# Twelve V-cache loads issued from the ACT queue in place of the SP queue, in a decode attention kernel

## The chip, the cores and the metric

The kernel runs on one core of a Trainium2 chip. The metric is the device time of one execution in microseconds (us). "Span" is the profiled execution's own length, some 1.7 us less than its time.

## The reference, cut to what matters

```python
def _A_ref(x, k_cache, v_cache, wq, wo):          # one token, 32 query heads on 4 KV heads
    q = (x @ wq) ...                              # wq 1024 x 4096
    scores = einsum(q, repeat(k_cache, 8)) * 128 ** -0.5    # caches 4 x 65536 x 128, bf16
    o = einsum(softmax(scores), repeat(v_cache, 8))
    return o @ wo
# ... B is an MLP with w1, w2 (1024 x 1024), w3 (1024 x 3584), w4 (3584 x 1024)
return x + _A_ref(xn, ...) + _B_ref(xn, ...)
```

The two caches are 67.1 MB each and every byte is read once. With the weights, 169.87 MB come from HBM for one token.

## The kernel before: the parts that matter

K and V are read in 16 blocks each (K0 to K15, V0 to V15) of 4 MiB, 128 partitions x 32 KiB, into two buffers each (`Kn`, `Vn`). A block serves two of the 32 steps. A third buffer, `W`, takes one weight load at a time. Every load but that of x (2 KB, from ACT) is issued by SP, in program order; each issue waits until the compute has freed the buffer.

```python
def issue_kv(t, b_t, cache, m, ch):
    ...
    s = m % 2
    src = cache[0, h, ...].rearrange("(p c) d -> p (c d)", p=P)
    if m < NPAIR - 1:
        _dma(q_sp, chan(...), lambda e: e.dma_start(out=t[:, s, :], in_=src), writes=b_t[s])
    else: ...                                     # the last block comes in two halves
...
for n in range(NT):                               # 32 steps
    QK(n)                                         # PE
    Ttr(n + 1, [0])                               # DVE transposes a quarter of the next K half block
    stats1(n); ...; EXP(n)                        # DVE, ACT
    Ttr(n + 1, [1]); PTr(n); Ttr(n + 1, [2, 3])
    PV(n)                                         # PE; after an odd n its V buffer is free
    FLASH(n)                                      # ACT copies OT_ps, POOL accumulates
    if n in at_pe:
        at_pe[n]()                                # n = 3, 7, ..: weight matmuls; after 3 and 15 a gelu,
                                                  # which has a tanh on ACT
    if n in at_dma:
        at_dma[n]()                               # n = 0, 4, 8, ..: next weight load
    if n % 2 == 0:
        issue_k(n // 2 + 2)
    else:
        issue_v(n // 2 + 2)
```

DVE works in order, so `Ttr(n + 1, [0])` before `stats1(n)` holds an odd step n until the next K block has landed. And each engine's queue works in order: a load issued from a queue goes out only when everything before it in that queue has been dispatched (seen below: V9 goes out at 239.72 us, together with the tanh before it).

## Time and profile before

| | before |
|---|---|
| time, median | 403.76 us |
| span | 401.9 us |
| bytes | 169.87 MB |
| DVE, PE, ACT busy | 57%, 48%, 12% |
| mean rate over the span | 423 GB/s |

From the profile page of the kernel before, parts 2 and 3. The first two lines cut the span into 40 slices: busy share of the 16 DMA engines in tenths, and GB/s. The last is the queue of the SP ring: packets, MB, share of the 16 engines' span.

```profile
DMA  8999999999999999999999999999999999999994
GB/s 356 427 416 436 444 421 419 450 432 421 444 434 423 432 434 439 416 434 452 423 420 450 426 424 444 432 421 435 430 435 427 445 430 424 424 431 430 436 419 205
...
q1 hardware_dynamic: 6920, 169.87, 98.4%
```

The engines are full from the second slice to the last but one. The table by stretches shows the same for two stretches (columns: stretch, its length, busy time of each engine, granted clock, DMA share, GB/s):

```profile
core 0: us, PE busy (x) PEld busy (x) DVE busy (x) ACT busy (x) POOL busy (x), PEclk, DMA share, GB/s
88.00:100.00 12.00, 4.85 (x39) 1.30 (x35) 8.99 (x17) 1.87 (x5) 1.98 (x2) 1.00 1.00 430
228.00:260.00 32.00, 20.17 (x172) 8.86 (x171) 21.89 (x40) 4.53 (x12) 4.38 (x5) 0.55 1.01 434
```

DVE does wait for K, by the list of waits (engine, line, tile, whom it waited for: us in total, times, longest):

```profile
DVE X L464 <- DMA Kn<-in_A_k_cache_dram: 64.2, 11, 9.9
```

While it waits, the DMA engines are not idle. This is a kernel bound by the bytes, and the compute merely waits its turn.

### The profile page before, as it was taken

What the parts mean: (1) busy time and instruction counts of PE and PEld (TensorE: products, weight loads), DVE (VectorE), ACT (ScalarE), POOL (GpSimd) and SP (SyncE); (2) the same over time, 40 slices, a digit from 0 to 9 for tenths busy, and PEclk for the clock granted to TensorE, in tenths of its full rate; (3) what the DMA queues carried; (4) which work ended last, traced back from release to release, by engine and by line L of the source; (5) the groups of instructions that cost most, each with busy time, mean ns of one, the idle gap of its engine ahead of it and who ended that gap; (6) DMA issues with size and microseconds to landing.
All of it is one profiled execution on the core that took longest, in us unless ns stands there. A gap on an engine that the chain in (4) does not pass through costs nothing.

```text
span 401.9 us, 5169 instructions
## 1 busy us (share of the span) xinstructions
PE 193.7 (48%) x2059; PEld 83.0 (21%) x2059; DVE 227.8 (57%) x400; ACT 48.3 (12%) x127; POOL 61.8 (15%) x90
## 2 busy tenths in 40 slices
PE   0361446064525756286640965454443645445645
PEld 0250111021103511062110731121111311111232
DVE  0217666277816588255753388576836775788410
ACT  0000201012101011011110011111201111111200
POOL 5000013011211011110310102111110112112110
PEclk9999999999955565555565556565565855665686
DMA  8999999999999999999999999999999999999994
GB/s 356 427 416 436 444 421 419 450 432 421 444 434 423 432 434 439 416 434 452 423 420 450 426 424 444 432 421 435 430 435 427 445 430 424 424 431 430 436 419 205
DMA packets 7088, 170.20 MB, mean 423 GB/s; under 512 B 916, under 2 KB 920, under 8 KB 1048
## 3 DMA queue, kind: packets, MB, share of 16 engines
q1 hardware_dynamic: 6920, 169.87, 98.4%
q8 instruction: 16, 0.26, 0.2%
q14 instruction: 8, 0.07, 0.0%
q10 hardware_dynamic: 144, 0.00, 0.0%
HBM read 169.87 MB, written 0.00 MB: 423 GB/s over the span
## 4 chain that ended last, share of the span: by engine, by line
DMA 54%; DVE 22%; PE 17%; ACT 3%; issue 2%; SPq 0%; POOL 0%; ACTq 0%
DMA Kn<-in_A_k_cache_dram 43%; DVE X L464 11%; DMA Kn<-in_B_w_dram 6%; DMA Vn<-in_A_wq_dram 5%; PE H_ps L367 4%; DVE pT_f L517 3%; PE S_ps L476 3%; PE OT_ps L524 3%; DVE mrow L483 3%; ACT p_sb L506 3%; PE M_ps L367 2%; PE PT_ps L515 2%; PE M_ps L552 1%; PE OUT_ps L392 1%; DVE Yall L381 1%
## 5 line engine op out<-in xcount | busy, mean ns | idle before, releaser
L464 DVE STREAM_TRANSPOSE X<-Kn 128x1024 f32<-128x1024 f32 x128 | 151.7, 1215 | 64.2 <-DMA Kn<-in_A_k_cache_dram 64.2
L524 PE MATMUL OT_ps<-Vn,pT_f 128*32 128x512 bf16 x512 | 59.9, 620 | 27.2 <-DVE pT_f L517 27.2
L476 PE MATMUL S_ps<-X,Yall 128*32 128x512 bf16 x512 | 57.5, 593 | 17.0 <-DVE X L464 17.0
L489 PE MATMUL MB_ps<-Rm,Lmat 128*128 128x16 bf16 x32 | 6.1, 192 | 87.3 <-DVE Rm L484 87.3
L538 POOL TENSOR_TENSOR O_acc<-O_acc,tmpO 128x513 f32<-128x513 f32 x28 | 32.9, 1174 | 89.0 <-ACT tmpO L532 89.0
L506 ACT ACTIVATE p_sb<-S_ps,brun 128x512 bf16<-128x512 f32 x32 | 22.0, 687 | 172.3 <-DVE brun L504 153.8
L536 POOL TENSOR_SCALAR O_acc<-O_acc,ff 128x513 f32<-128x513 f32 x28 | 19.5, 698 | 149.8 <-ACT ff L511 149.8
L515 PE MATMUL PT_ps<-p_sb,permR 128*128 128x512 bf16 x32 | 18.2, 568 | 39.7 <-ACT p_sb L506 39.7
L483 DVE TENSOR_REDUCE mrow<-S_ps 128x1 f32<-128x512 f32 x32 | 21.6, 674 | 24.2 <-PE S_ps L476 24.2
L532 ACT ACTIVATE tmpO<-OT_ps 128x512 f32<-128x512 f32 x32 | 19.1, 598 | 107.6 <-PE OT_ps L524 107.6
L476 PEld LDWEIGHTS S_ps<-X,Yall 128*32 128x32 bf16 x512 | 16.5, 125 | 54.8 <-DVE X L464 38.6
L517 DVE STREAM_TRANSPOSE pT_f<-PT_ps 128x512 f32<-128x512 f32 x32 | 22.9, 716 | 7.6 <-PE PT_ps L515 7.6
L524 PEld LDWEIGHTS OT_ps<-Vn,pT_f 128*32 128x32 bf16 x512 | 14.5, 127 | 59.2 <-DVE pT_f L517 42.4
L489 PEld LDWEIGHTS MB_ps<-Rm,Lmat 128*128 128x128 bf16 x32 | 3.3, 102 | 111.2 <-DVE Rm L484 111.2
L367 PEld LDWEIGHTS H_ps<-xn_bf,W 128*128 128x128 bf16 x224 | 14.4, 174 | 1.7 <-issue 1.7
L367 PE MATMUL H_ps<-xn_bf,W 128*128 128x1 bf16 x224 | 14.5, 202 | 0.0
L515 PEld LDWEIGHTS PT_ps<-p_sb,permR 128*128 128x128 bf16 x32 | 3.4, 106 | 42.4 <-ACT p_sb L506 42.4
L493 DVE TENSOR_REDUCE Bst<-MB_ps 128x1 f32<-128x16 f32 x32 | 5.6, 174 | 8.3 <-PE MB_ps L489 8.3
L331 PE MATMUL M_ps<-ln_s,ones_f 128*128 128x1 f32 x6 | 1.8, 363 | 17.5 <-DVE ln_s L330 17.5
L534 POOL COPY O_acc<-tmpO 128x513 f32<-128x513 f32 x4 | 2.4, 612 | 47.6 <-ACT tmpO L532 47.6
L392 PE MATMUL OUT_ps<-Kn,gh_bf 128*1 128x256 bf16 x112 | 6.4, 402 | 5.5 <-DMA Kn<-in_B_w_dram 5.5
L619 DVE CAST orow<-OUT_ps 128x256 bf16<-128x256 f32 x1 | 0.4, 425 | 13.2 <-PE OUT_ps L392 13.2
(101 smaller groups left out, 117.3 us busy)
## 6 DMA issues: line engine op xcount, KB each, us to landing
Kn<-in_A_k_cache_dram SPq DMA_DIRECT2D x15, 4096.0 KB, 27.5
Vn<-in_A_v_cache_dram SPq DMA_DIRECT2D x15, 4096.0 KB, 22.2
W<-in_B_w_dram SPq DMA_DIRECT2D x2, 3584.0 KB, 24.9
W<-in_A_wo_dram SPq DMA_DIRECT2D x3, 2048.0 KB, 24.3
Kn<-in_A_wq_dram SPq DMA_DIRECT2D x1, 4096.0 KB, 12.2
Vn<-in_A_wq_dram SPq DMA_DIRECT2D x1, 4096.0 KB, 21.4
W<-in_B_w_dram SPq DMA_DIRECT2D x2, 2048.0 KB, 32.1
Kn<-in_A_k_cache_dram SPq DMA_DIRECT2D x2, 2048.0 KB, 24.9
```

The costliest lines, as they stand in the source:

```text
L367: fns.append(lambda e, j=j, cx=cx: e.matmul(ps_tile[:, c0 + cx:c0 + cx + 1], lhs_fn(j - j0, cx), rhs_fn(j), start=(j == 0 and cx == 0), st ...
L392: fns.append(lambda e, lhs=lhs, rhs=rhs, jj=jj: e.matmul(OUT_ps[32 * jj:32 * jj + 1, 0:256], lhs, rhs[:, 256 * jj:256 * jj + 256], start=F ...
L464: _op(q_dve, lambda e, ix=ix: e.transpose(out=X32[:, xs, 1024 * ix:1024 * (ix + 1)], in_=Kn32[:, s, 4096 * half + 1024 * ix:4096 * half + ...
L476: fns.append(lambda e, we=we, cm=cm, mv=mv: e.matmul(S_ps[32 * cm:32 * cm + 32, :], Yall[:, h, we, :, :].rearrange("p a g -> p (a g)"), mv ...
L483: _op(q_dve, lambda e: e.reduce_max(mrow[:, m:m + 1], S_ps[:, :], axis=AX.X), reads=[b_S], writes=[b_mrow[m]])
L506: _op(q_act, lambda e: e.activation(p_sb[:, m, :], S_ps[:, :], ACTF.Exp, bias=brun[:, kn:kn + 1], scale=SCALE, accum_out=tmpO[:, m, 512:513]),
L515: _op(q_pe, lambda e: e.matmul(PT_ps[:, :], permR[:, :], p_sb[:, m, :], start=True, stop=True), reads=[b_p[m], b_const], writes=[b_PT])
L517: _op(q_dve, lambda e: e.transpose(out=pT_f[:, :], in_=PT_ps[:, :]), reads=[b_PT], writes=[b_pT])
L524: fns.append(lambda e, q=q, q4=q4: e.matmul(OT_ps[32 * q4:32 * q4 + 32, :], pT_bf[:, q, :, 1], Vn[:, s, 8192 * half + 512 * q:8192 * half ...
L532: _op(q_act, lambda e: e.activation(tmpO[:, m, 0:512], OT_ps[:, :], ACTF.Copy), reads=[b_OT], writes=[b_tmpO[m]], partial=True)
L536: _op(q_pool, lambda e: e.tensor_scalar(out=O_acc[:, :], in0=O_acc[:, :], scalar1=ff[:, m:m + 1], scalar2=0.0, op0=ALU.mult, op1=ALU.add), ...
L538: _op(q_pool, lambda e: e.tensor_tensor(out=O_acc[:, :], in0=O_acc[:, :], in1=tmpO[:, m, :], op=ALU.add), reads=[b_tmpO[m]], writes=[b_Oacc])
```

## The change

The intent was to have two rings of loads feed each DMA engine, in the hope that the engine finds work in one ring while the other is between loads. V2 to V13 go to ACT's queue; the first and last V blocks, all of K and all weights stay on SP.

```diff
-        def issue_kv(t, b_t, cache, m, ch):
+        def issue_kv(t, b_t, cache, m, ch, q=None):
+            q = q or q_sp
...
-                _dma(q_sp, chan("%s%d" % (ch, s)), ...)
+                _dma(q, chan("%s%d" % (ch, s)), ...)
...
-            issue_kv(Vn, b_V, A_v_cache, m, "v")
+            issue_kv(Vn, b_V, A_v_cache, m, "v", q_act if 2 <= m < NPAIR - 2 else q_sp)
```

More of the change, by code (lines that the diff above doesn't have):

```diff
@@ L286, in issue_kv @@
             if m < NPAIR - 1:
-                _dma(q_sp, chan("%s%d" % (ch, s)), lambda e: e.dma_start(out=t[:, s, :], in_=src), writes=b_t[s])
+                _dma(q, chan("%s%d" % (ch, s)), lambda e: e.dma_start(out=t[:, s, :], in_=src), writes=b_t[s])
             else:
```

## The prediction

> **What bounds the kernel now.** The 16 DMA engines. The table of stretches shows a DMA share of 1.00 and 432 GB/s in every stretch from 10 to 300 us; the page shows queue q1 (the SP ring) with 169.87 MB and 98.4% of the engines' span. No compute engine is near that (DVE 57%, PE 48%). In the packet records a 32 KiB packet takes 1213 ns at the median, the 5th and the 95th percentile, a 16 KiB packet 611 ns: 9 ns plus bytes at 27.2 GB/s per engine, 435 GB/s for 16. That is the 435 GB/s that the Trainium skill ("DMA: Bandwidth & Descriptors", Specifications) gives as the fabric ceiling; this trace agrees. The bytes alone need 169.87 MB / 432 GB/s = 393 us of the 402 us span; the rest is about 3 us of start and 4 us after the last loads.
>
> The SP ring is never short of work: by the timeline's issue times and sizes, at each issue 6.9 us (at 241 us) to 32 us of transfer are still queued. DVE's waits for K in the list of waits (64.2 us, 11 times) are full engines, not late issues.
>
> **What the change removes, adds, moves.** 12 loads of 4 MiB, 50.3 MB or 30% of the bytes, move to ACT's ring (q10), with 12 issues of 0.33 us. ACT is busy 12%; an issue stands right after the copy of OT_ps, which already waited for the PV that frees the V buffer, so ACT waits for nothing new, and its idle 3.3 us or more before the next exponential take up the 0.33 us. Nothing is removed from the 393 us.
>
> *Gain possible:* a second ring can hide at most the 9 ns per packet, 0.7% of the shared stretch, under 2 us. The same page ("Issuing engines are not separate DMA queues") says that DMAs of several issuers run on the same 16 engines and interleave, saving only sequencer time. I expect that.
>
> *Loss possible:* K no longer has the engines alone, and V is fetched before it is needed. With equal sharing (my estimate from 432 GB/s, the issue order, 8.1 us per step and the measured weight-matmul extras) K lands some 6 us later relative to the bytes moved, most of all behind a W load; the issues that hang on K come later and the queued reserve shrinks by as much. Its minimum near 241 us, and the end near 370 us, then come close to zero, with perhaps 1 us of idle engines in all. The last flash step ends some 4 us later (381 now); PE has about 5 us of slack before the last W4 load at 399 us, so this stays hidden, just.
>
> **On the critical path:** nearly nothing: the bytes and the rate per engine stay.
>
> **Prediction: 404.0 us, range 401.5 to 408.5.** Faster by over 2%: 0.02; within 2%: 0.92; slower by over 2%: 0.06.
>
> **What the profile would show.** q10 with about 50 MB, q1 about 119.5; 428 to 436 GB/s from 10 to 360 us; 32 KiB packets of two rings that take about twice 1213 ns or alternate at 1213; DVE waits for K still 60 to 75 us, single ones over 10 us after a W load; V landing before it is needed.
>
> **What would make it wrong.** Packets of two rings that together exceed 27.2 GB/s per engine (faster); a switching cost per packet: 50 ns would be 4% of the shared stretch (slower); unfair sharing, K far below half, which empties both rings while compute waits (slower); a compute end more than 5 us later.

## More of the kernel before

Last, the timeline of the kernel before around V9's issue, lines of other work left out (start, length, engine, line, operation, in brackets the idle time before it and its releaser):

```profile
221.67 1.90 PE L524 MATMUL OT_ps<-Vn,pT_f 128*32 128x512 bf16 x16 [0.81 <-DVE pT_f L517]
223.50 7.26 PE L367 MATMUL H_ps<-xn_bf,W 128*128 128x1 bf16 x112
223.62 0.60 ACT L532 ACTIVATE tmpO<-OT_ps 128x512 f32<-128x512 f32 x1 [3.33 <-PE OT_ps L524]
223.68 0.33 SPq L287 DMA_DIRECT2D Vn<-in_A_v_cache_dram  x1
231.68 0.23 ACT L412 ACTIVATE ge_a<-ge_b 128x28 f32<-128x28 f32 x1 [7.46 <-DVE ge_b L411]
```

V9 goes out at 223.68 us, right after the PV of step 15 has freed its buffer. The weight matmul (7.26 us) and the tanh of the gelu come after it.

## The result, and the profile after

The changed kernel takes 413.53 us (median of 5 runs, 411.90 to 414.02), the kernel before 403.76 us (5 runs, 403.68 to 404.60). The ratio is 1.0232, 95% interval 1.0211 to 1.0253: slower. The profiled run has a span of 410.2 us, 8.3 us more than before. It is the fastest of the five (411.90 us); the median run is 1.6 us longer, and no trace of it was kept.

The same lines of the page, after:

```profile
DMA  8999999998999999999999969999999999999994
GB/s 358 409 457 407 447 419 441 430 438 318 435 428 441 416 429 431 447 419 433 432 428 436 419 268 414 455 412 430 434 446 425 414 412 435 409 425 432 449 414 206
...
q1 hardware_dynamic: 5192, 119.54, 68.3%
q10 hardware_dynamic: 1872, 50.33, 28.7%
```

The bytes moved to q10 as intended. Two slices stand out, the tenth (318 GB/s) and the 24th (268 GB/s). The table by stretches:

```profile
88.00:100.00 12.00, 6.53 (x99) 3.01 (x99) 9.05 (x23) 1.90 (x6) 1.79 (x2) 0.50 0.82 325
228.00:260.00 32.00, 22.36 (x223) 12.84 (x224) 21.18 (x39) 4.01 (x12) 4.19 (x5) 0.55 0.88 369
```

The DMA engines, which were never idle before, now run dry: the share falls from 1.00 to 0.82 and from 1.01 to 0.88. Adding up the bytes of the packet records per microsecond against 432 GB/s, what was not moved amounts to 2.6 us at 94 to 98 us, 4.3 us at 235 to 241 us, and 1.3 us in three smaller places (near 190, 329 and 339 us): 8.2 us in all, out of the 8.3 us that the span grew. So in this run that sum is where the time went. The rate of a busy engine did not change: a 32 KiB packet still takes 1213 ns at the median and at the 5th and 95th percentile, on either ring.

Three more views say how the engines came to run dry. First, the chain that ended last, the piece for K2 (start, length), before and then after:

```profile
49.95 27.53 DMA Kn<-in_A_k_cache_dram
```

```profile
49.87 37.02 DMA Kn<-in_A_k_cache_dram
```

K2 is issued at the same time (49.9 us) and lands 9.4 us later. Second, the wait of DVE for K after the change: fewer waits, and the longest doubled.

```profile
DVE X L465 <- DMA Kn<-in_A_k_cache_dram: 72.6, 8, 18.8
```

The longest is the wait for K2, by the timeline:

```profile
86.91 1.25 DVE L465 STREAM_TRANSPOSE X<-Kn 128x1024 f32<-128x1024 f32 x1 [18.81 <-DMA Kn<-in_A_k_cache_dram]
```

Third, the timeline around V9's issue, after, with the same lines left out:

```profile
229.71 1.90 PE L525 MATMUL OT_ps<-Vn,pT_f 128*32 128x512 bf16 x16 [0.81 <-DVE pT_f L518]
231.54 7.26 PE L368 MATMUL H_ps<-xn_bf,W 128*128 128x1 bf16 x112
231.66 0.60 ACT L533 ACTIVATE tmpO<-OT_ps 128x512 f32<-128x512 f32 x1 [3.33 <-PE OT_ps L525]
238.88 0.33 SPq L447 DMA_DIRECT2D W<-in_A_wo_dram  x1
239.72 0.23 ACT L413 ACTIVATE ge_a<-ge_b 128x28 f32<-128x28 f32 x1 [7.45 <-DVE ge_b L412]
239.72 0.33 ACTq L288 DMA_DIRECT2D Vn<-in_A_v_cache_dram  x1
```

The PV that frees V9's buffer ends at 231.6 us, but the issue stands behind the tanh in ACT's program and goes out with it at 239.72 us, 8.1 us late. V3 stands behind the tanh of the first gelu in the same way: ACT's copy is at 93.89 us, the tanh at 96.47, the issue at 96.48. On SP neither had to wait for a tanh. Both late issues fall in the two stretches that run dry. That suggested the first theory below. Alone it turned out not to be enough.

### How the shares of the rings can be read

The packet records tell how many bytes each ring moved. In GB/s, from the changed kernel and from three experiments that are described below:

| kernel | stretch, us | waiting on SP (row) | on ACT (row) | SP ring | ACT ring | SP's share |
|---|---|---|---|---|---|---|
| after | 66 to 70 | W1 (16 KiB) | V2 (32 KiB) | 133.5 | 297 | 0.31 |
| after | 76 to 80 | K2 (32 KiB) | V2 (32 KiB) | 246 | 187 | 0.57 |
| k_halves_first | 74 to 76 | K2 (16 KiB) | V2 (32 KiB) | 139 | 294 | 0.32 |
| halves_first | 76 to 80 | K2 (32 KiB) | V2 (16 KiB) | 300 | 132 | 0.69 |
| quarters_first | 76 to 80 | K2 (32 KiB) | V2 (8 KiB) | 334 | 98 | 0.77 |

The sum stays at 430 to 433 GB/s, but the shares follow the row sizes: 16 against 32 KiB gives about a third, equal rows about a half, 32 against 8 KiB about four fifths. (The 0.57 for equal rows is over a half because V2's last packets start between 75.6 and 79.2 us: on some engines the ACT ring ran empty within the stretch.) The Trainium skill ("DMA: Bandwidth & Descriptors", section "Queues, rings and completion order") says that each engine takes turns between the queue rows it has work for, a whole packet at a time. This trace agrees, with a turn here as large as one row of the load. A ring with smaller rows is therefore served with fewer bytes.

K2's own lateness does not come from these shares. Its 9.4 us are nearly the whole transfer of V2 (4 MiB at 432 GB/s, 9.7 us): V2's last packet ends at 80.5 us, before K2 lands at 86.9, so V2, W1 and K2 had all been moved by then, and at equal shares K2 would have landed no earlier. Halving K's rows moves it as little: in k_halves_first, where K takes half of V's turn, K2 lands at 86.9 us too. Only shares that leave part of V2 unmoved help it, as in quarters_first, where it lands at 81.7 us.

The packet records show one more thing about a ring that was empty. When the other ring still has much queued, the first packet of a new load starts 3.4 to 4.1 us after its issue (V2: issued at 59.96, first packet at 63.44 us; V8: 209.25 and 212.72); when the engines have run dry, it starts after 0.95 to 0.98 us. Why is not shown.

### The profile page after: what moved, and what is told of

Same layout as the page of the kernel before. It is cut to its first block, busy times and chain, and to the rows that moved or that the text cites. A ratio compares the mean times of both kernels' runs of the same rounds, so it can differ in the third digit from the quotient of the medians.

```text
span 410.2 us, 5141 instructions
## 1 busy us (share of the span) xinstructions
PE 185.1 (45%) x2043; PEld 82.8 (20%) x2059; DVE 227.8 (56%) x400; ACT 48.3 (12%) x127; POOL 61.8 (15%) x90
## 4 chain that ended last, share of the span: by engine, by line
DMA 51%; DVE 25%; PE 18%; issue 2%; ACT 2%; another core or an unknown queue 1%; SPq 0%; POOL 0%; ACTq 0%
DMA Kn<-in_A_k_cache_dram 40%; DVE X L465 13%; DMA Kn<-in_B_w_dram 5%; DMA Vn<-in_A_wq_dram 5%; PE S_ps L477 4%; PE H_ps L368 4%; DVE pT_f L518 3%; DVE mrow L484 3%; PE OT_ps L525 3%; PE M_ps L368 2%; ACT p_sb L507 2%; PE PT_ps L516 1%; PE M_ps L553 1%; PE OUT_ps L393 1%; DVE Rm L485 1%
## 5 line engine op out<-in xcount | busy, mean ns | idle before, releaser
L465 DVE STREAM_TRANSPOSE X<-Kn 128x1024 f32<-128x1024 f32 x128 | 151.3, 1214 | 72.6 <-DMA Kn<-in_A_k_cache_dram 72.6
L516 PE MATMUL PT_ps<-p_sb,permR 128*128 128x512 bf16 x16 | 9.1, 566 | 21.2 <-ACT p_sb L507 21.2
L553 PE MATMUL M_ps<-O_acc,cb_W 128*128 128x128 f32 x32 | 6.5, 364 | 2.0 <-DVE cb_W L546 2.0
```

The lines of the kernel that those rows point to most:

```text
L465: _op(q_dve, lambda e, ix=ix: e.transpose(out=X32[:, xs, 1024 * ix:1024 * (ix + 1)], in_=Kn32[:, s, 4096 * half + 1024 * ix:4096 * half + ...
L516: _op(q_pe, lambda e: e.matmul(PT_ps[:, :], permR[:, :], p_sb[:, m, :], start=True, stop=True), reads=[b_p[m], b_const], writes=[b_PT])
L553: fns.append(lambda e, t=t: e.matmul(M0_ps[:, 128:256], cb_W[:, t, :, :].rearrange("p g i -> p (g i)"), O_acc[:, t * P:(t + 1) * P], start ...
```

## The experiments

All against the kernel before, run beside it on the same chip. The diffs shown are against the changed kernel, except that of one_ring_late. "Not moved" is the sum described above, between 40 and 345 us, of the profiled run.

| run | time, median us | ratio to before (95% interval) | span, us | not moved, us |
|---|---|---|---|---|
| before | 403.7 to 403.9 | 1 | 401.9 | 0 |
| after | 413.53 | 1.0232 (1.0211 to 1.0253) | 410.2 | 8.2 |
| v_first | 410.88 | 1.0177 (1.0162 to 1.0192) | 409.2 | 6.7 |
| v9_first | 408.87 | 1.0123 (1.0108 to 1.0138) | 407.1 | 4.5 |
| one_ring_late | 403.98 | 1.0008 (0.9993 to 1.0023) | 402.9 | 0.6 |
| v_halves | 407.33 | 1.0086 (1.0069 to 1.0103) | 405.7 | 3.8 |
| act_only | 403.77 | 0.9996 (0.9980 to 1.0013) | 402.3 | 0 |
| halves_first | 406.10 | 1.0048 (1.0027 to 1.0069) | 404.8 | 1.3 |
| quarters_first | 405.37 | 1.0035 (1.0018 to 1.0052) | 403.6 | 0 |
| k_halves_first | 413.17 | 1.0242 (1.0212 to 1.0272) | 411.6 | 8.6 |
| early_halves | 406.67 | 1.0069 (1.0054 to 1.0084) | 404.5 | 2.2 |
| w_act | 407.15 | 1.0093 (1.0053 to 1.0134) | 405.4 | 2.9 |
| halves_from3 | 404.30 | 1.0014 (0.9997 to 1.0031) | 402.3 | 0 |

One of the four runs of quarters_first was slow (413.39 us, with no lower granted clock than the others; why is not known) and is left out of its ratio. Outputs were correct in all runs.

### First set: late issue or shared engines?

Theory 1: the loss comes from the late issues of V3 and V9 behind the tanh, on a reserve of queued loads that sharing has made thin. Theory 2: the sharing alone is enough. Theory 3: two rings make packets slower.

**v_first**: V is issued before the weight matmuls of its step.

```diff
+            if n % 2 == 1:
+                issue_v(n // 2 + 2)
             if n in at_pe:
                 at_pe[n]()
...
-            else:
-                issue_v(n // 2 + 2)
```

> The changed kernel with each V load issued before the weight matmuls and the gelu of its step instead of after them, so that the loads of V3 and V9 no longer stand behind a tanh in ACT's order (96.48 and 239.72 us in the changed kernel, where the PV that frees the buffer ended at 93.8 and 231.6). Theory 1 (late issue behind the tanh, on a reserve that sharing has thinned): the idle of the DMA engines at 94 to 98 us and 235 to 241 us nearly goes, 404 to 406.5 us, DMA share 0.99 to 1.00 in both stretches. Theory 2 (the sharing of the engines between K and V alone delays K and starves the rings; the tanh is beside the point): unchanged, 411 to 414 us. Theory 3 (two rings make packets slower): unchanged too.

Measured: 410.88 us. It lies between the theories: the lateness is gone (V3 at 93.96, V9 at 235.52 us, the tanhs at 96.54 and 243.58), but only 2.65 of the 9.8 us come back. The two stretches in v_first:

```profile
88.00:100.00 12.00, 6.52 (x99) 3.00 (x99) 9.06 (x23) 1.83 (x6) 1.79 (x2) 0.50 0.97 396
228.00:260.00 32.00, 20.39 (x207) 12.36 (x208) 21.00 (x40) 3.95 (x11) 3.11 (x4) 0.50 0.90 370
```

The first is mended in part (325 to 396 GB/s). In the second one idle place has become two, at 234 to 238 and 251 to 255 us, with 2.2 and 2.6 us not moved. Theory 1 falls as the whole explanation.

**v9_first**: only V9 is issued early (`if n == 15: issue_v(...)` before `at_pe`; the others stay).

> Only V9 is issued before the weight matmul and gelu of step 15; V3 stays behind its tanh. Theory 1: the idle near 238 us (about 4.4 us worth of bytes) goes and the one near 96 us (about 2.6 us) stays: 407.5 to 410 us. Theories 2 and 3: 411 to 414 us.

Measured: 408.87 us, inside theory 1's range, and in the places that it named: the one at 94 to 98 us stayed (2.8 us), the one at 235 to 241 us is gone, and 1.7 us are left from 230 us on. V9 now goes out right after ACT's copy:

```profile
232.61 0.60 ACT L533 ACTIVATE tmpO<-OT_ps 128x512 f32<-128x512 f32 x1 [3.33 <-PE OT_ps L525]
232.62 0.34 ACTq L288 DMA_DIRECT2D Vn<-in_A_v_cache_dram  x1
```

And yet it is faster than v_first, which mends V3 as well. With V3 late the later blocks met each other in a different order: K8 landed at 225.6 us with 11.0 us queued, against 228.5 us and 6.6 us in v_first. How much is lost in one place depends on the phases of K, V and the weights, and does not add up change by change.

**one_ring_late**: the kernel before, with the same lateness put in.

```diff
         def issue_v(m):
+            if m in (3, 9):
+                q_sp.wait(tanh_ev[0])      # the event of the gelu's tanh
```

> The kernel before (all loads on the SP ring) with the same lateness put in: SP waits for the tanh before it issues V3 (2.5 us later) and V9 (8 us later). Theory 1 says both parts are needed: the one ring still held 10.5 us of transfer at V3's issue and 9.6 us at V9's, more than the delays, so the engines stay busy: 403.5 to 405 us, DMA share 1.00 in 90 to 100 and 220 to 250 us. If lateness alone is the cause, whatever the rings: 408 us or more.

Measured: 403.98 us, 0.6 us not moved. On one ring 8 us of lateness costs next to nothing: V9 went out at 231.8 us with 2.0 us of transfer still queued, as the sum said (10.1 us queued when it goes out on time, less 8.1).

**v_halves**: the order of the changed kernel, but each V load on ACT is two loads of 16 KiB rows, so that V's turn is half of K's.

```diff
+            if q is q_act:
+                for hf in range(2):
+                    _dma(q, chan(...), lambda e, hf=hf: e.dma_start(out=t[:, s, 8192 * hf:8192 * hf + 8192],
+                         in_=src[:, 8192 * hf:8192 * hf + 8192]), writes=[b_t[s][hf]])
```

> The changed kernel, order kept (V3 and V9 behind the tanh), but each V load of the ACT ring cut into two loads of 16 KiB rows, so that a turn of the ACT ring is 16 KiB and one of the SP ring 32 KiB for K and 16 KiB for W: K should get about two thirds of the engines while both rings hold work, and W a half in place of a third. Theory 2: most of the loss goes, 404 to 406.5 us. Theory 1: K lands earlier, so the reserve is larger, but V3 and V9 are as late: a part goes, 406 to 410 us. Theory 3: unchanged or slower (about 1 us for 96 more packets per engine at 9 ns).

Measured: 407.33 us: a part goes, though the late issues stay. Tilting the turns alone gives back 6.2 of 9.8 us, more than taking away the lateness does (2.65 us in v_first, 4.7 us in v9_first).

So the four corners are: one ring, 403.7 us; one ring with late issues, 404.0; two rings with timely issues, 410.9; two rings with late issues, 413.5. Lateness costs 0.2 us on one ring and 2.6 us on two. Sharing with timely issues costs 7.1 us. By these corners theory 2 has the larger part. The split is not a firm one, though: v9_first, with V3 still late, is 5.1 us above the kernel before, so mending V9 alone gives back 4.7 of the 9.8 us. What is shown is that lateness costs next to nothing without sharing, and that sharing costs several us without lateness. Theory 3 falls by the packets, which take 1213 ns as before.

### Second set: is it the sharing, and which way?

Theory A: two rings share each engine, K lands later and less is queued when the next issue is due. Theory B: ACT as the issuer costs.

**act_only**: K2 to K13, V2 to V13 and the weight loads between them all go on ACT's ring, in the old order, V issued first in its step.

```diff
-            issue_kv(Kn, b_K, A_k_cache, m, "k")
+            issue_kv(Kn, b_K, A_k_cache, m, "k", q_act if 2 <= m < NPAIR - 2 else q_sp)
...
+                wq[0] = q_act if n >= 4 else q_sp     # queue of the weight loads
                 at_dma[n]()
+                wq[0] = q_sp
```

> K and V blocks 2 to 13 and the weight loads between them all go on the ACT ring, in the order of the kernel before (V issued before the weight matmuls of its step); the rest stays on SP. One ring holds nearly everything again, but it is ACT that issues. Theory A (what costs is that two rings share each engine: K lands with less queued behind it, 6.6 to 14.9 us of transfer against 12 to 22 before, and the next load cannot be issued until 7 us after K lands): back to the time before, 403.5 to 405.5 us. Theory B (the cost lies in ACT as the issuer, its in-order queue or its ring): stays at 409 us or more.

Measured: 403.77 us, ratio 0.9996. ACT issues 30 loads in place of 13, and nothing is lost:

```profile
88.00:100.00 12.00, 7.22 (x80) 2.34 (x77) 9.23 (x18) 1.68 (x5) 1.98 (x2) 0.50 1.01 436
228.00:260.00 32.00, 20.71 (x176) 9.15 (x175) 21.91 (x40) 4.54 (x12) 4.39 (x5) 0.55 1.01 433
```

Theory B falls: issuing from ACT, or using its ring, is not what costs. Having two rings is.

**halves_first**: v_first and V in two loads of 16 KiB rows.

> Both mends at once: V issued first in its step, and each V load of the ACT ring cut into two of 16 KiB rows so that K gets two thirds of the engines while both rings hold work. Theory A: K lands earlier, more stays queued at its landing; better than either alone, 404.5 to 407 us. If the turns of the rings are not what matters: as v_first, 410 to 411.5 us.

Measured: 406.10 us, inside the range, with 1.3 us not moved.

**quarters_first**: the same with four loads of 8 KiB rows.

> The same with V in four loads of 8 KiB rows: K gets about four fifths. Theory A: K about as early as on one ring, at the cost of about 2.5 us for 288 more packets per engine at 9 ns each, part of it off the idle time; V now comes last and PV may wait for it (it did, 21 us in all, in v_halves): 405 to 408.5 us.

Measured: 405.37 us, and nothing is left unmoved; the rest over the kernel before is about the cost of the added packets. By the fit of 9 ns plus bytes at 27.2 GB/s, 288 more packets per engine are 2.6 us (an estimate from the packet durations of the kernel before); the span grew by 1.7.

**k_halves_first**: the opposite tilt. K's loads on SP are cut into two of 16 KiB rows (compute waits for both), V stays whole.

> The opposite tilt, on v_first: each K load of the SP ring cut into two of 16 KiB rows (compute still waits for both), V kept at 32 KiB, so that V gets two thirds. Theory A: K lands later still, less stays queued, more idle engines than v_first: 412 to 419 us. If only the number of rings or the extra packets matter: 410.5 to 412 us.

Measured: 413.17 us, inside theory A's range though near its lower end:

```profile
88.00:100.00 12.00, 6.52 (x99) 3.00 (x99) 9.05 (x23) 1.82 (x6) 1.79 (x2) 1.00 0.99 395
228.00:260.00 32.00, 19.53 (x192) 11.90 (x192) 19.39 (x38) 3.95 (x11) 3.10 (x4) 0.50 0.91 376
```

With V issued in time in all four, the time follows K's turn against V's: 413.2 us at 1:2, 410.9 at 1:1, 406.1 at 2:1, 405.4 at 4:1, and 403.8 on one ring. Cutting loads costs packets in each of the three cut kernels, so it is the tilt that separates them.

### Third set: what is left

**early_halves**: as halves_first, but the first half of a V block is issued a step earlier, as soon as its half of the buffer is free.

> As halves_first (V in two loads of 16 KiB rows on the ACT ring, before the weight matmuls), but the first half of a V block is issued one step earlier, as soon as the PV of its first half frees the buffer. The sharing is that of halves_first; only the reserve grows: half a V block (2 MiB, 4.9 us of transfer) can already be queued when K lands. Theory A (idle engines come from a thin reserve at K's landing): the rest of the idle (1.3 us at 94 to 100 in halves_first) goes, 403.5 to 405 us. If the remaining 2.3 us of halves_first are a cost of two rings or of more packets themselves: stays at 405.5 to 406.5 us.

Measured: 406.67 us, a miss. The idea was to have more queued when K lands. But an early V half is also more V in front of K: K2 landed at 92.0 us in place of 85.9 in halves_first, with 7.9 us queued against 9.1, and 2.2 us were not moved against 1.3. On two rings a load issued earlier takes turns from the one that is waited for.

**w_act**: v_first with the weight loads moved to ACT's ring too.

> v_first (whole V loads of 32 KiB rows on ACT, issued first), with the weight loads moved to the ACT ring as well, so that K is alone on the SP ring and no weight load stands in front of it. Theory A: K no longer waits behind a weight load that gets only a third to a half of the engines, so it lands earlier with more queued: 404.5 to 408 us against 410.9 for v_first. If the equal turns of K and V alone make the loss: 410 to 412 us.

Measured: 407.15 us (one run 409.67), inside theory A's range; so about half of what v_first loses has to do with the weight loads being on K's ring. Moving them also puts them in front of V, and this run cannot tell the two apart. K2 was not helped, though: it landed at 87.0 us all the same, with 8.0 us queued, which is less than K3 alone, so V2 and W1 had both been moved before it; and PE now waited 40.9 us for V, six times.

**halves_from3**: halves_first with V2 back on SP (`3 <= m` in place of `2 <= m`).

> halves_first with V2 back on the SP ring, so that V2 no longer takes two thirds to a half of the engines while W1 and K2 wait on SP. Theory A: K2 lands at about 77.5 us as in the kernel before (not 85.9), 17 us of transfer stay queued at its landing, and the idle of 1.3 us at 94 to 100 us, the only one left in halves_first, goes; what then remains over the kernel before is about 1 us for 88 more packets per engine: 404.3 to 405.5 us. If two rings cost by themselves: 406 us as halves_first.

Measured: 404.30 us, ratio 1.0014 (0.9997 to 1.0031). K2 lands at 77.3 us with 17.8 us queued, and the last idle place is gone. So two rings can be tuned until they cost about nothing. No version of them beat the kernel before, and neither did one ring on ACT.

### The sum that gives the idle time

Why does late K make the engines run dry, when the bytes are the same? Because the next issue hangs on K. After K lands, DVE transposes, and it is 7.0 us until PV has ended and V's next load can be issued (K2 lands at 86.9 us, ACT's copy that follows PV starts at 93.89). With the engines dry, the first packet starts 0.95 to 0.98 us after an issue. So at K's landing some 8 us must be queued (an estimate from these two), or another issue must come meanwhile. The landings come from the semaphore records, "queued" is bytes issued less bytes moved, at 432 GB/s:

| kernel | K lands, us | queued, us | queue ends, us | next issue, us | its first packet, us | not moved, us |
|---|---|---|---|---|---|---|
| before, K2 | 77.5 | 17.6 | 95.1 | V3 at 84.5 | (not idle) | 0 |
| before, K8 | 216.6 | 17.1 | 233.7 | V9 at 223.7 | (not idle) | 0 |
| after, K2 | 86.9 | 8.2 | 95.1 | W2 at 95.71 | 96.66 | 2.6 |
| after, K8 | 224.7 | 11.9 | 236.6 | wo0 at 238.88 | 239.85 | 4.3 |
| v_first, K8 | 228.5 | 6.6 | 235.1 | V9 at 235.52 | 236.50 | 2.2 |

(The engines finish and start about a microsecond apart from each other, so the lost bytes do not equal the gap exactly.) One row does not run dry for want of reserve alone: after, K8 has 11.9 us queued, more than 8. There V9 could have gone out at 231.66 us, with ACT's copy and some 5 us still queued; it is the tanh, 8.1 us later, that let the engines run dry. On one ring K8 had 17.1 us queued, and the same lateness cost 0.6 us (one_ring_late). Before, with everything in one ring in the order of need, K lands with V of the same block and the next K both still to come: 17 us. With two rings, V has been moved while K was on its way, and that much less is left. Put in one number, the least transfer that was queued at any issue between 45 and 350 us: 7.4 us before, none in the changed kernel and in v_first, 2.1 us in halves_first, 6.7 us in halves_from3.

## Why the prediction was wrong, point by point

- **What bounds the kernel, and the rate**: right. The bytes at 432 GB/s bound it, a second ring hid nothing of a packet's 1213 ns, and packets of two rings alternate with the same sum. The prediction drew here on the Trainium skill ("DMA: Bandwidth & Descriptors", section "Issuing engines are not separate DMA queues"); the trace agrees: 430 to 433 GB/s with both rings busy.
- **Direction of the loss**: the mechanism was named. K lands later relative to the bytes, the queued reserve shrinks, worst behind a weight load and near 241 us. K2's single wait went to 18.8 us ("over 10 us after a W load"), and the sum of the waits, 72.6 us, lies in the stated 60 to 75.
- **The step that failed: "with perhaps 1 us of idle engines in all."** It measured 8.2 us. Timely issues on two rings alone (v_first) leave 6.7 us. The prediction counted the reserve at issues on one ring (its least was 6.9 us, 7.4 us by the count used here) and subtracted a delay of K of some 6 us. That delay was mis-sized where it mattered: relative to the bytes moved, K2 landed 9.5 us later, all of V2, while K8 landed 5.2 us later. The reserve that matters is the one at K's landing, against the 7.0 us of compute and 0.96 us of first packet until the next load can start. The stretch at 94 to 98 us, which K2 makes dry, was not seen at all. Sharing was also taken as equal in bytes, whereas a ring with 16 KiB rows got 0.31 of the bytes against 32 KiB rows; for K2 this made no difference, as said above.
- **A second step that failed: "so ACT waits for nothing new."** That holds for ten of the twelve loads. V3 and V9 stand behind the gelu's tanh in ACT's order and went out 2.6 and 8.1 us after PV. Undoing this gives 2.65 us (413.53 to 410.88), and undoing it for V9 alone 4.7 us (v9_first, 408.87). The order of instructions per engine, which was there to be read, shows both.
- **The end**: right that it stays hidden. The changed kernel's span grew by 8.3 us, and 8.2 us of that are unmoved bytes before 345 us.
- **Time**: 404.0 us predicted, range 401.5 to 408.5, measured 413.53. The chance given to "slower by over 2%" was 0.06. One of the listed causes of an error, rings that both run empty while compute waits, is what happened; the share needed for it was not "far below half", as K2 had 0.57 once it stood at the head of its ring.

What stays open: how the losses divide between single places. v9_first beat v_first though it mends less, and no run explains each later place one by one.

## What to carry to other kernels

When the DMA engines are full, as here, a second ring brings no bandwidth (430 to 433 GB/s with both rings busy, 432 with one); it only changes the order in which bytes arrive, from the order of need to taking turns. Keep loads that the compute waits for next ahead of loads that it needs later, and check how much transfer is queued when the awaited load lands against the time until the next issue can follow. If a load must go on a compute engine's queue, look at what stands before it in that engine's program, and remember that a load with smaller rows got the smaller share here (0.31 for 16 KiB beside 32 KiB).

## What the Trainium skill lacked or had wrong

- "DMA: Bandwidth & Descriptors", rules for kernel authors: it says that spreading loads over several issuers does not help. It does not say that it can cost: 403.76 to 413.53 us with the same bytes, of which 5.1 to 7.1 us remain when V9 or all V loads are issued in time (v9_first, v_first).
- The same page, "Queues, rings and completion order": turns go by packet, but nothing is said of shares. Here they followed the row size of the load: 0.31 for 16 KiB against 32 KiB rows, about a half (0.57) for equal ones, 0.77 for 32 against 8 KiB.
- The same page, Specifications: first-byte latency of about 0.6 us for loads issued from SP or ACT; the row does not say from when it counts. With idle engines the first packet's record starts 0.95 to 0.98 us after the start of the issuing instruction, and 0.63 to 0.65 us after its end (it takes 0.33 us), so the figure agrees if counted from the end. Behind a busy other ring the first packet comes 3.4 to 4.1 us after the issue, for which the page has no figure.
- The same page, Specifications: about 27 GiB/s per engine. The packets here give 27.0 GB/s for 32 KiB rows (1213 ns), which agrees with that page's 435 GB/s for 16 engines and not with 27 GiB/s.
